# One transfer for each token tile of the first half, and tile 1's statistics ahead of tile 0's normalization

## The chip, the core and the metric

The kernel runs on one NeuronCore of one Trainium2 chip. The core has a matrix engine (TensorE, PE in the profile; its weight loads are the row PEld), a vector engine (VectorE, DVE), an activation engine (ScalarE, ACT), a general engine (GpSimd, POOL) and a queue engine that only issues transfers (SyncE, SP). ACT and POOL can issue transfers too. All transfers run on 16 shared DMA engines between HBM and SBUF, the on-chip memory of 128 partitions. PSUM holds matmul results. Every engine works through its own list in order; between engines there are semaphores. The metric is device time of one execution in microseconds (us), the median of the runs.

## What is computed

The input `x` has 2048 tokens of 576 values. Each token is normalized, and the result goes through two branches that are added to `x`: a long convolution whose kernel comes from a state-space model, and a feed-forward block with 4608 hidden units.

```python
x = A_u                                   # (1, 2048, 576)
xn = _layernorm(x, axis=-1)               # (x - mean) / sqrt(var + 1e-5), no weights
return x + _A_ref(xn, A_re, A_im, B_re, B_im, C_re, C_im, log_dt, Dskip) + _B_ref(xn, w1, w2)

def _B_ref(x, w1, w2):
    h = jnp.einsum("bsd,df->bsf", x, w1)  # 576 -> 4608
    h = _silu(h)
    return jnp.einsum("bsf,fd->bsd", h, w2)

# _A_ref: K[d, l] = Re sum_n C * exp(dt * A * l) * dt * B, for l = 0..2047;
#         y = causal convolution of xn with K along the tokens (by FFT), plus xn * Dskip
```

All of it is fp32. The kernel splits each operand of a matmul into a high and a low part (`h` and `l` in the names) and takes three products.

## The kernel before

**Tokens.** The tokens stand in 16 tiles of 128, tile j being `x` at 16 values of the rest. On the way in, tile j puts token 64n + 32·q2 + 16·q1 + j on partition 32·(2·q1 + q2) + n. The views `xv` and `ov` have that layout in four quarters of 32 partitions, so a load (`load_x`) or a store (`store`) of a tile, or of a pair of tiles, is four transfers of 32 partitions. The convolution's first stage needs just this order of the partitions: it reads the normalized tokens back from the DRAM buffer `dxn` (`xr<-dxn` in `spread`, line 146), and `dxn` is filled from the `xn` tiles by GpSimd (line 240). The feed-forward branch treats each token alone and needs no order.

**Stages.** `ffn` is the main stream. For half 0 (tiles 0 to 7) and half 1 (tiles 8 to 15) it runs over 9 chunks of four 128-wide pieces of the hidden units: `up` (lines 311 to 313, `ph`) makes 512 tokens by 128 hidden units, ScalarE applies silu (`gf`, line 319) and casts the high part (`gh`, line 320), VectorE makes the low part (`gl`, line 321), and `down` (line 341, `po`) multiplies by w2; VectorE adds the result into `acc` (line 346). `acc` of a tile is the loaded tile itself, so the residual is in it. Most of half 1 runs in a form with fewer products (line 468). `side` is woven between: it normalizes the tiles, prepares the state-space tables (`natural`, `kgen`; inputs `are`, `aim`, `cr` and so on), spreads the tokens (`spread`), multiplies in the transformed domain (`spectral`) and ends the convolution.

**The first 50 us.** Tile 0 and tile 1 are loaded by eight transfers, from SP and ACT in turn. `norm` takes statistics on VectorE (`st`, line 188; `mv`, line 189), adds 1e-5 to the variance (`sd`, line 192), GpSimd raises that to the power -1/2 (line 193), and VectorE or, for odd tiles from 5 on, ScalarE (line 202) writes `xn`. `turned` transposes `xn` on TensorE (`pt`, lines 122 and 127), and ScalarE and VectorE split the transposed tile into `xh`/`xl` (lines 123 and 125) and the small `x` piece (lines 128 and 129). Tiles 0 to 3 are block 0, tiles 4 to 7 block 1. An `up` product of a block reads all of that block's columns, except that the first one is cut into two halves of 256 columns, tiles 0 and 1 first. The tiles `xn` live in a pool `pa`, which is closed after tile 7: whatever is allocated there next, above all the state-space inputs `dt`, `are`, ... (loaded by SP from line 684 on), waits until the transfers out of `xn` have landed and TensorE has read the last tile.

**What sets the order.** Each engine's order is made when the program is built: a scheduler places the instructions by a simulated timeline, in the order of the code as `weave` mixes it and with `tc.high_priority()` ahead. `behind(ins)` places an instruction on its engine after another one. The first transfers of SP and ACT share eight completion semaphores; a ninth such transfer is issued only when the first has landed, and so on round. GpSimd's transfers have eight of their own.

```python
for i in range(n):
    for h in range(2):
      with behind(pins["xn"] if js[0] == 1 else None):
        nc.vector.bn_stats(out=st[:, i, h, :], in_=xs[i][:, h * HD:(h + 1) * HD])
```

So tile 1's statistics stand behind `pins["xn"]`, the instruction that writes tile 0's `xn`.

## Time and profile before

| | |
|---|---|
| median of 3 runs | 1107.37 us (1106.05 to 1108.47) |
| profiled execution | 1108.0 us, its span 1106.1 us (the rest lies around the span) |
| TensorE busy | 1089.5 us, 98% |
| TensorE weight loads | 986.5 us, 89% |
| VectorE busy | 950.6 us, 86% |
| ScalarE busy | 722.6 us, 65% |
| GpSimd busy | 141.5 us, 13% |
| HBM read / written | 109.64 MB / 62.60 MB |
| granted TensorE clock | 0.999 |

The span runs from the first instruction to the last. A row of the timeline has the start in us, the length in us, the engine (SPq and ACTq are the queues that issue transfers), the line, the operation, output<-input, and in brackets how long the engine had been idle and what ended that. In a table of stretches, each engine's busy time is followed by its number of instructions; then come the clock, the DMA engines' busy share and GB/s. A row of waits says who waited for whom: us in total, times, and the longest.

### The profile page before, as it was taken

Reading aid. Unit: us, or ns where it says so; the run is one execution under the profiler, and the core shown is the slowest. Engines: PE = TensorE matmul, PEld = TensorE weight load, DVE = VectorE, ACT = ScalarE, POOL = GpSimd, SP = SyncE. Lnnn points to the kernel's source line nnn. Section 1 sums busy time; section 2 is a strip of 40 time slices with the busy share of each in tenths; the row PEclk is TensorE's granted clock in tenths of the full one; section 3 lists DMA queues with packets and bytes.
Section 4 is the critical chain, followed back from the end, with each engine's and each line's share of the span. In section 5 each row is a group of like instructions: output and inputs, shape, how many; then the busy total and the mean of one; then the engine's idle time right before and its main releaser. Section 6 shows DMA issues by size and latency. Waiting matters only on the chain.

```text
span 1106.1 us, 23074 instructions
## 1 busy us (share of the span) xinstructions
PE 1089.5 (98%) x9101; PEld 986.5 (89%) x9101; DVE 950.6 (86%) x1615; ACT 722.6 (65%) x1283; POOL 141.5 (13%) x246
## 2 busy tenths in 40 slices
PE   6999999999999999999999999999999999999998
PEld 5989999898998888898999899999999998999787
DVE  6699989999999999999999997988888888886323
ACT  4475457677777676767667656877778777785320
POOL 1112100000000000000330001111111111111220
PEclk9999999999999999999999999999999999999999
DMA  8536552355263535457974246456545655554984
GB/s 261 157 123 205 168 165 94 118 149 153 84 176 108 138 125 132 154 120 254 240 196 89 84 92 193 146 167 179 158 152 176 182 173 150 177 161 109 248 216 111
DMA packets 163100, 173.67 MB, mean 157 GB/s; under 512 B 88608, under 2 KB 128816, under 8 KB 162352
## 3 DMA queue, kind: packets, MB, share of 16 engines
q1 hardware_dynamic: 137360, 105.02, 34.6%
q0 software_dynamic: 24272, 65.38, 19.4%
q10 hardware_dynamic: 1360, 1.80, 0.7%
q8 instruction: 72, 1.18, 0.5%
q14 instruction: 36, 0.29, 0.1%
HBM read 109.64 MB, written 62.60 MB: 156 GB/s over the span
## 4 chain that ended last, share of the span: by engine, by line
PE 78%; DVE 12%; ACT 3%; DMA 3%; issue 2%; SPq 0%; POOL 0%; ACTq 0%; DVEq 0%
PE po L341 34%; PE ph L311 16%; PE pb L468 6%; PE pc L468 3%; PE kp L888 2%; PE pk L1022 2%; PE pb L1022 2%; PE pu L1022 2%; PE pa L468 2%; PE ph L313 1%; PE ph L312 1%; PE z L903 1%; DMA kl<-d1k 1%; DVE acc L346 1%; DVE th L829 1%
## 5 line engine op out<-in xcount | busy, mean ns | idle before, releaser
L341 PE MATMUL po<-w,gh 128*128 128x288 f32 x2304 | 474.3, 296 | 0.7 <-DVE acc L346 0.7
L341 PEld LDWEIGHTS po<-w,gh 128*128 128x128 f32 x2304 | 375.1, 188 | 16.6 <-issue 3.3
L341 PE MATMUL po<-w,gl 128*128 128x288 f32 x1152 | 333.5, 295 | 0.0
L341 PEld LDWEIGHTS po<-w,gl 128*128 128x128 f32 x1152 | 214.9, 188 | 1.7
L346 DVE TENSOR_TENSOR acc<-po,acc 128x288 f32<-128x288 f32 x296 | 129.8, 451 | 54.5 <-PE po L341 53.2
L311 PE MATMUL ph<-xh,w1h 128*128 128x512 f32 (+1 forms) x368 | 99.7, 388 | 1.4 <-ACT gf L319 1.0
L311 PE MATMUL ph<-xl,w1h 128*128 128x512 f32 (+1 forms) x368 | 98.2, 384 | 0.0
L311 PE MATMUL ph<-xh,w1l 128*128 128x512 f32 (+1 forms) x368 | 98.0, 383 | 0.0
L319 ACT ACTIVATE gf<-ph 128x512 f32<-128x512 f32 (+1 forms) x92 | 53.0, 579 | 51.3 <-PE ph L313 31.5
L311 PEld LDWEIGHTS ph<-xl,w1h 128*128 128x128 f32 x368 | 68.0, 191 | 13.4
L311 PEld LDWEIGHTS ph<-xh,w1l 128*128 128x128 f32 x368 | 66.6, 189 | 12.0
L311 PEld LDWEIGHTS ph<-xh,w1h 128*128 128x128 f32 x368 | 65.0, 191 | 11.7 <-ACT gf L319 1.6
L845 ACT ACTIVATE c<-th,magic 128x1040 f32<-128x1040 f32 x36 | 42.0, 1168 | 40.6 <-DVE C L866 26.5
L159 POOL DMA_DIRECT2D d1u<-u x32 | 17.6, 550 | 393.9 <-ACT u L158 392.5
L847 ACT ACTIVATE c<-th 128x1040 f32<-128x1040 f32 x36 | 38.7, 1074 | 40.7 <-DVE th L846 40.6
L321 DVE TENSOR_TENSOR gl<-gf,gh 128x512 fp32r<-128x512 f32 (+1 forms) x92 | 60.3, 658 | 3.8 <-ACT gh L320 3.6
L927 POOL DMA_DIRECT2D m<-in_cm_dram x64 | 34.0, 533 | 216.0 <-PE pu L1022 135.8
L320 ACT CAST gh<-gf 128x512 fp32r<-128x512 f32 (+1 forms) x92 | 55.1, 602 | 8.7 <-PE po L341 7.7
L485 DVE TENSOR_TENSOR gl<-gf,gh 128x512 fp32r<-128x512 f32 x56 | 37.8, 688 | 23.4 <-ACT gh L484 23.0
L865 DVE TENSOR_TENSOR S<-th,C 128x1024 f32<-128x1024 f32 x36 | 43.8, 1218 | 7.4 <-ACT th L848 7.3
L846 DVE SCALAR_TENSOR_TENSOR th<-c,th 128x1040 f32<-128x1040 f32 x36 | 44.3, 1232 | 0.3 <-ACT c L845 0.3
L829 DVE TENSOR_TENSOR th<-vt,fT 128x1040 f32<-128x1040 f32 x36 | 44.3, 1233 | 0.2
(269 smaller groups left out, 2371.0 us busy)
## 6 DMA issues: line engine op xcount, KB each, us to landing
w1r<-in_B_w_dram SPq DMA_DIRECT2D x35, 512.0 KB, 3.9
dw<-w SPq DMA_DIRECT2D x28, 576.0 KB, 4.8
w<-dw POOLq DMA_DIRECT2D x28, 576.0 KB, 5.9
w2r<-in_B_w_dram SPq DMA_DIRECT2D x44, 288.0 KB, 4.8
d1u<-u POOLq DMA_DIRECT2D x32, 288.0 KB, 2.9
d1k<-stage SPq DMA_DIRECT2D x18, 512.0 KB, 6.5
ul<-d1u SPq DMA_DIRECT2D x32, 288.0 KB, 3.0
kl<-d1k SPq DMA_DIRECT2D x32, 288.0 KB, 3.6
```

Source lines behind the costliest of these rows:

```text
L311: nc.tensor.matmul(ph, w[:, kt, :], v[:, kt, a:e], start=n + kt == 0, stop=False)
L319: nc.scalar.activation(gf, ph, AF.Silu)
L320: pins["gh"] = nc.scalar.copy(gh, gf).ins
L321: pins["gl"] = nc.vector.tensor_sub(gl, gf, gh).ins
L341: pins["pe"] = nc.tensor.matmul(po[:, :HD], gs[g][:, js], ws[:, w, hs], start=n == 0 and j not in begun, stop=n == 3 * len(terms) - 1, ski ...
L346: nc.vector.tensor_add(acc[j][:, hs], po[:, :HD], acc[j][:, hs])
L468: pins["pe"] = nc.tensor.matmul(dst, a[:, kt], v[:, kt], start=start and n == 0, stop=stop and n == 5, skip_group_check=True).ins
L829: nc.vector.tensor_mul(split(th), row(vt[:, 0:65], 65), col(fT, i, 65))
L845: nc.scalar.activation(c65, th, AF.Identity, bias=magic)
L846: nc.vector.scalar_tensor_tensor(th, c65, MAGIC, th, op0=ALU.subtract, op1=ALU.subtract)
L865: nc.vector.tensor_mul(ov3, t[:, :, 0:64].rearrange("n d (x y) -> n d x y", y=32), mv3)
L1022: nc.tensor.matmul(dst, st, mv[:, hs], start=n == 0, stop=n == 3 * len(terms) - 1)
```

## The change

- Tiles 0 to 7 get another layout, `xw` and `ow`: partition p of tile j holds token 16p + j. A load of tile 0 or 1, and of each pair (2, 3), (4, 5), (6, 7), is then one transfer of 128 partitions, and so is each store of those pairs at the end of half 0. Tile 0 comes by SP, tile 1 by ACT. Tiles 8 to 15 keep the quarters.
- Since `dxn` keeps its order of partitions, the copy of `xn` of these tiles into `dxn` becomes four transfers of 32 partitions, each from every fourth partition of `xn`.
- Tile 1's statistics stand behind `pins["var"]`, the instruction that adds 1e-5 to tile 0's variance.

```diff
+    xw = x.rearrange("b (p j) d -> p (b j) d", j=NJ)
+    ow = out.rearrange("b (p j) d -> p (b j) d", j=NJ)
...
         t = pool.tile([P, 2, D], F32, tag=tag, name=f"{tag}{j}")
-        for i in range(j, j + 2, 1 if j == 0 else 2):
+        if j == 0:
+            for i, eng in enumerate(engines):
+                eng.dma_start(t[:, i], xw[:, i])
+        elif j < 8:
+            nc.sync.dma_start(t, xw[:, j:j + 2])
+        else:
             for ps, v, eng in quarters(xv, engines):
-                if j == 0:
-                    eng.dma_start(t[ps, i], v[:, i])
-                else:
-                    eng.dma_start(t[ps], v[:, j:j + 2])
+                eng.dma_start(t[ps], v[:, j:j + 2])
...
-              with behind(pins["xn"] if js[0] == 1 else None):
-                nc.vector.bn_stats(out=st[:, i, h, :], in_=xs[i][:, h * HD:(h + 1) * HD])
+                with behind(pins["var"] if js[0] == 1 else None):
+                    nc.vector.bn_stats(out=st[:, i, h, :], in_=xs[i][:, h * HD:(h + 1) * HD])
...
-        nc.vector.tensor_scalar(sd[:, :n], mv[:, :n, 1], 1e-5, None, op0=ALU.add)
+        pins["var"] = nc.vector.tensor_scalar(sd[:, :n], mv[:, :n, 1], 1e-5, None, op0=ALU.add).ins
...
-        held.append((dxn[:, js[0]:js[0] + len(js)], xn[:, :len(js)]))
+        ds = dxn[:, js[0]:js[0] + len(js)]
+        if js[0] < 8:
+            held.extend((ds[32 * q:32 * q + 32], xn[2 * (q % 2) + q // 2::4, :len(js)]) for q in range(4))
+        else:
+            held.append((ds, xn[:, :len(js)]))
...
-                    store(pairs[j - 1], j - 1, (nc.gpsimd,))
+                    nc.gpsimd.dma_start(ow[:, j - 1:j + 1], pairs[j - 1])
```

The order of the instructions moves with it on every engine, since the scheduler places them anew. Line numbers of the changed kernel are up to 9 higher than those before. Three places follow.

On VectorE, at the very start, the rows of tile 0 and tile 1 before (`st`, `mv`, `sd`, `xn` as above; `acc_104` is the pair of tiles 0 and 1):

```order
L188 BN_STATS st<-acc_104 128x6 x2
L189 BN_AGGR mv<-st 128x2
L192 TENSOR_SCALAR sd<-mv 128x1
L197 TENSOR_SCALAR xn<-acc_104,mv,sd 128x576
L188 BN_STATS st<-acc_104 128x6 x2
L189 BN_AGGR mv<-st 128x2
```

and with the change:

```order
L193 BN_STATS st<-acc_104 128x6 x2
L194 BN_AGGR mv<-st 128x2
L197 TENSOR_SCALAR sd<-mv 128x1
L193 BN_STATS st<-acc_104 128x6 x2
L202 TENSOR_SCALAR xn<-acc_104,mv,sd 128x576
L194 BN_AGGR mv<-st 128x2
```

The two statistics of tile 1 have moved ahead of tile 0's `xn`; the rest stands as it was.

On TensorE, at the end of block 0's first `down` products, where tile 7 is transposed (`pt`; the row of 64x128 is its last piece) and block 1's first `up` product (`ph<-xh`) follows, before:

```order
L122 MATMUL pt<-ident,xn 128x128 x4
L341 MATMUL po<-w_240,gh 128x288 x2
L341 MATMUL po<-w_240,gl 128x288
L341 MATMUL po<-w_243,gh 128x288 x2
L127 MATMUL pt_338<-ident,xn 64x128
L341 MATMUL po<-w_243,gl 128x288
L341 MATMUL po<-w_246,gh 128x288 x2
L341 MATMUL po<-w_246,gl 128x288
L341 MATMUL po<-w_249,gh 128x288 x2
L341 MATMUL po<-w_249,gl 128x288
L311 MATMUL ph<-xh_273,w1h 128x512 x8
```

and with the change:

```order
L350 MATMUL po<-w_246,gh 128x288 x2
L350 MATMUL po<-w_246,gl 128x288
L350 MATMUL po<-w_249,gh 128x288 x2
L350 MATMUL po<-w_249,gl 128x288
L125 MATMUL pt<-ident,xn 128x128 x4
L130 MATMUL pt_335<-ident,xn 64x128
L320 MATMUL ph<-xh_270,w1h 128x512 x8
```

Before, twelve products stood between the four large transposes of tile 7 and block 1's first `up`; now only the small transpose does.

On GpSimd, the transfers out of `xn` between the powers (`sd`) of the pairs, before:

```order
L193 TENSOR_TENSOR sd<-sd,mhalf 128x2
L240 DMA dxn<-xn 128x576 x2
L240 DMA dxn<-xn 128x1152
L193 TENSOR_TENSOR sd<-sd,mhalf 128x2 x2
L240 DMA dxn<-xn 128x1152 x2
```

and with the change:

```order
L198 TENSOR_TENSOR sd<-sd,mhalf 128x2
L249 DMA dxn<-xn 32x576 x8
L249 DMA dxn<-xn 32x1152 x4
L198 TENSOR_TENSOR sd<-sd,mhalf 128x2 x2
L249 DMA dxn<-xn 32x1152 x8
```

Five transfers have become twenty, twelve of them ahead of the powers of tiles 4 to 7.

## The prediction

> **What bounds the kernel now.** I read the page's busy times first, then a table of stretches to find where TensorE is not busy, then the timeline and the waits at those places.

> ```profile
> PE 1089.5 (98%) x9101; PEld 986.5 (89%) x9101; DVE 950.6 (86%) x1615; ACT 722.6 (65%) x1283; POOL 141.5 (13%) x246
> ...
> 0.00:12.00 12.00, 3.58 (x14) 2.67 (x15) 5.34 (x17) 4.50 (x9) 2.05 (x7) 1.00 0.72 204
> 12.00:30.00 18.00, 16.90 (x125) 16.22 (x125) 16.15 (x42) 9.51 (x24) 2.62 (x4) 1.00 1.01 294
> 62.00:80.00 18.00, 17.45 (x104) 15.57 (x103) 17.41 (x30) 13.66 (x16) 4.17 (x5) 1.00 0.42 140
> 300.00:400.00 100.00, 99.14 (x1076) 88.93 (x1075) 97.76 (x143) 70.84 (x105) 3.79 (x7) 1.00 0.52 148
> ```

> TensorE is the bound. It idles 16.6 us of 1106.1 (span less 1089.5): 8.4 in the first 12, 1.1 from 12 to 30, 0.55 from 62 to 80, 0.86 from 300 to 400. So the change can gain at most a part of the first 8.4, and what it delays counts only where TensorE then stands. From 300 to 400 VectorE has 2.2 us of air in 100: a wait there would reach TensorE soon.

> **The start, part by part.** This is the chain up to the first `up` product.

> ```profile
> 0.75 1.79 SPq L169 DMA_DIRECT2D acc<-in_A_u_dram  x4
> 3.37 0.40 SPq L257 DMA_DIRECT2D w1r<-in_B_w_dram  x1
> ...
> 4.29 0.82 DVE L188 BATCH_NORM_STATS2 st<-acc 128x6 f32<-128x288 f32 x2 [3.36 <-DMA acc<-in_A_u_dram]
> 5.39 0.15 DVE L192 TENSOR_SCALAR sd<-mv 128x1 f32<-128x1 f32 x1
> 6.24 0.58 DVE L197 TENSOR_SCALAR xn<-acc,mv,sd 128x576 f32<-128x576 f32 x1 [0.69 <-POOL sd L193]
> 6.73 0.81 DVE L188 BATCH_NORM_STATS2 st<-acc 128x6 f32<-128x288 f32 x2
> 7.58 0.21 DVE L189 BATCH_NORM_AGGREGATE mv<-st 128x2 f32<-128x12 f32 x1
> 8.66 0.58 DVE L197 TENSOR_SCALAR xn<-acc,mv,sd 128x576 f32<-128x576 f32 x1 [0.68 <-POOL sd L193]
> 9.59 0.72 ACT L279 CAST w1h<-w1r 128x640 fp32r<-128x640 f32 x1 [0.82 <-DMA w1r<-in_B_w_dram]
> 10.45 0.59 ACT L123 CAST xh<-pt 128x512 fp32r<-128x512 f32 x1
> 11.08 0.58 PE L311 MATMUL ph<-xh,w1h 128*128 128x256 f32 x1 [0.46 <-ACT xh L123]
> ```

> *Load.* Tile 0 is there just before 4.29. One transfer of 288 KB does not stand in this trace at this place; the nearest row is `xr<-dxn`, which also reads 128 rows of 2304 bytes with the same step of 36,864 bytes. The rows below it are DMA rates: the quarters of tiles 0 and 1, the quarters of tiles 2 and 3 (10.5 to 12.5 us), and whole 128-partition loads of w2 (13.5 to 15.5).

> ```profile
> DMA to landing us min/median/max: 2.7/3.7/10.8
> ...
> 1.50:4.50 3.00, 0.00 (x0) 0.00 (x0) 0.21 (x1) 1.19 (x2) 0.50 (x1) 1.00 0.78 221
> 10.50:12.50 2.00, 1.54 (x7) 1.42 (x7) 1.37 (x3) 2.00 (x5) 0.00 (x0) 1.00 0.95 249
> 13.50:15.50 2.00, 2.00 (x13) 2.00 (x13) 2.00 (x5) 0.00 (x0) 0.00 (x0) 1.00 1.03 338
> ```

> Early end: the 2.7 us, so tile 0 lands at 0.75 + 2.7 = 3.45. Late end: tile 1's 295 KB goes through at the same time from the other queue; at 221 GB/s that adds 1.33 us, so 4.78. If the median 3.7 holds instead of 2.7, it is 5.78. Against a landing of about 4.15 now, that is 0.7 earlier, 0.6 later, or 1.6 later. I take the middle of the first two, 4.1: the whole loads of w2 move faster (338) than quarters (249), which speaks for the early half, and the sharing for the late one. So the load as such gives 0.07.

> [...]

> *Statistics.* With 0.07 off, tile 0's variance is done at 5.47 (5.39 + 0.15 - 0.07). Tile 1's statistics, 0.81, run from 5.49 to 6.30 while GpSimd takes the power; it is done for VectorE at 6.17. Tile 0's `xn` so starts at 6.34 instead of 6.24, a loss of 0.1 that nothing waits for, since tile 1 is the later one. After it, at 6.95, tile 1's aggregation starts, 0.63 before its 7.58, and all behind it moves by 0.63: `xn` to 8.03, `xh` to 9.82, the first `up` to 10.45.

> *Weights.* ScalarE casts `w1h` between the two `xh`, and that cast waited for w1 until 9.59. It must start by 9.1. Its load stood behind the landing of a quarter (issued at 3.37, when a semaphore of the eight came free); with two transfers ahead instead of eight it needs no free semaphore and is issued some 2 us earlier on SP. I count that as enough; if w1 came no earlier, the gain would be 0.1.

> The start: -0.6 us, between -1.3 (early end) and +1.0 (5.78, less the 0.63).

> **Tile 7's transposes and the release of the pool.**

> ```profile
> 42.12 0.60 PE L122 MATMUL pt<-ident,xn 128*128 128x128 f32 x4
> 42.76 0.59 ACT L123 CAST xh<-pt 128x512 fp32r<-128x512 f32 x1 [2.59 <-PE pt L122]
> 43.53 0.26 ACT L128 CAST x<-pt 64x128 fp32r<-64x128 f32 x1 [0.18 <-PE pt L127]
> 43.57 0.31 SPq L684 DMA_DIRECT2D dt<-in_A_log_dt_dram  x1
> 44.26 2.00 PE L311 MATMUL ph<-xh,w1h 128*128 128x512 f32 x8
> 49.35 0.95 DVE L702 TENSOR_TENSOR aim<-aim,dt 96x768 f32<-96x768 f32 x1 [1.18 <-ACT aim L701]
> 51.13 0.41 PE L680 MATMUL ptk<-ident,aim 96*128 96x96 f32 x3
> ...
> SPq L684 <- DMA dxn<-xn: 8.0, 2, 6.6
> SPq L684 <- PE pt L127: 5.8, 1, 5.8
> ```

> Now twelve products run while ScalarE casts tile 7's `xh` (42.76 to 43.35). With the new order only the small transpose does, so `ph<-xh` stands still from about 42.75 to 43.39 of this clock: +0.6 us (0.5 to 0.7). Start and this cancel: TensorE begins block 1 at 44.26 as before.

> The release moves more. SP's `dt` load waits for two things, last of all for the read of tile 7: by the two rows the last `dxn` had landed 5.8 us before the transpose was done, at about 37.6. The cast of the small piece (43.53) then comes right behind `xh`, which ends 0.04 before 44.26, so `dt` goes out at about 44.2, 0.65 later. `aim` is ready for TensorE at 50.95 instead of 50.30, and wanted at 51.13: covered, with 0.18 left.

> ```profile
> 62.70 0.68 DVE L321 TENSOR_TENSOR gl<-gf,gh 128x512 fp32r<-128x512 f32 x1
> 63.31 0.95 DVE L730 TENSOR_TENSOR pi<-pi,t 96x768 f32<-96x768 f32 x1
> 64.29 0.85 ACT L733 ACTIVATE ci<-pi 96x768 f32<-96x768 f32 x1 [1.86 <-DVE pi L730]
> ...
> 77.63 1.20 PE L311 MATMUL ph<-xh,w1h 128*128 128x512 f32 x4 [0.56 <-ACT gf L319]
> ```

> From `ci` ScalarE works without a gap until the `gf` for which TensorE waits 0.56 at 77.63, so this chain carries the delay. But the new order has `pi` ahead of that `gl`: +0.65 - 0.61 = 0.04. So 77.63 stays where it is.

> **Transfers on GpSimd.** Fifteen more issues; the nearest price is that of 32-partition loads on the same queue.

> ```profile
> 17.87 1.99 POOL L240 DMA_DIRECT2D dxn<-xn  x3
> 17.95 1.07 DVE L197 TENSOR_SCALAR xn<-acc,mv,sd 128x576 f32<-128x576 f32 x2 [0.21 <-POOL sd L193]
> 30.07 1.62 POOL L193 TENSOR_TENSOR sd<-sd,mhalf 128x2 f32<-128x2 f32 x2 [10.21 <-DVE sd L192]
> 33.84 0.54 POOL L240 DMA_DIRECT2D dxn<-xn  x1 [0.32 <-ACT xn L202]
> ...
> L178 POOL DMA_DIRECT2D out_dram<-yt x16 | 12.6, 1208 | 33.8 <-ACT yt L991 33.8
> L171 POOL DMA_DIRECT2D acc<-in_A_u_dram x16 | 7.8, 495 | 15.1 <-DMA out_dram<-acc 15.1
> ...
> dxn<-xn POOLq DMA_DIRECT2D x2, 288.0 KB, 5.2
> ```

> Twelve from 17.87 at 0.5 end at 23.9; the next power is wanted at 30.07: hidden by 6 us. Eight from 33 end at 37, and with 5.2 to land at 42.2, before the release at 44.2. The cost is nothing while that cover of 2 us holds; the dearer price, 1.2 us of `yt`, is a rival below. At the end of half 0, twelve store issues fewer and whole loads elsewhere free queues that TensorE doesn't wait for: nothing.

> **Sum.** -0.6 + 0.6 + 0.04, and nothing for the new order behind 80 us, where the ends are -0.86 (the one idle there goes) and the +3.4 of the second rival: 0.0. The profiled execution took 1108.0, 1.9 more than its span and 0.6 more than the median; I forecast 1107.4 against the median 1107.37. A measurement of this kernel tells about 0.2%, 2.2 us, from no change. With the start's ends, this case reaches from 1105.8 (early end, and the idle of 300 to 400 gone) to 1109.0 (the latest landing).

> **Rivals.**
> 1. *The copies hold the release* (slower). If a 32-partition copy out of `xn` cost GpSimd the 1.2 us of `yt` (the same bytes and partitions), twelve would end at 32.4, 2.3 after the power at 30.07; eight more from 35.2 end at 44.9 and land at 50.1, 5.9 after 44.2. SP, VectorE and ScalarE would carry that to 77.63: 1113.3. It decides from a price of 0.75 us on (33 + 8 x 0.75 + 5.2 = 44.2). For it: `yt`'s price. Against: 0.495 for plain loads, 0.54 at 33.84, and `yt` accumulates. [...]
> 2. *The new order starves VectorE in the middle* (slower). Every engine's order after 80 us is new. If the 500 us from 140 to 640, where the tables keep VectorE full, each lost 0.86 per 100 as 300 to 400 does, that would be 4.3 instead of 0.86: +3.4, 1110.8. For it: 97.76 of 100. Against: the same work by the same scheduler. It decides from 2.2 lost.
> 3. *The start keeps its gain* (faster). Early end, -1.3; loads that move at 338 instead of 249 also take the 1.1 of 12 to 30 and the 0.55 of 62 to 80 with them; tile 7 still costs 0.6: -2.35, 1105.0. For it: DMA share 1.01 from 12 to 30. Against: TensorE's waits there are for VectorE and ScalarE, and 62 to 80 hangs on the release.

> **How the numbers follow.** No change that can be told: 0.62. Rival 1: 0.08, rival 2: 0.15, rival 3: 0.15. So faster 0.15, same 0.62, slower 0.23. The range 1105.0 to 1110.8 runs to rivals 3 and 2; rival 1 and the tails beyond the two, about 0.2, stay out.

> **What would show it.** Right: the first `up` at about 10.4, tile 1's statistics at 5.5 inside GpSimd's power, a TensorE idle of 0.6 ahead of block 1's `ph` caused by ScalarE's `xh`, `dt` at 44.2, and again about 0.5 idle at 77.6. Wrong: statistics of tile 0 later than 4.9 or earlier than 3.6; `dt` waiting last for `dxn`; copies above 0.75 us; more than 2 us of TensorE idle between 80 and 1000.

## The result, and the profile after

| | median us | lowest to highest | ratio to before |
|---|---|---|---|
| before, beside it | 1107.74 | 1106.05 to 1108.47 | |
| changed | 1115.51 | 1114.86 to 1116.43 | 1.0066 (1.0054 to 1.0079) |

The change makes the kernel 7.8 us slower. The forecast of 1107.4, with a range up to 1110.8, was wrong.

The profiled execution took 1115.5 us; its span is 1113.8, that is 7.7 more than before. First the busy times and the table of stretches of the changed kernel (busy time and number of instructions by engine, the granted clock of TensorE, the DMA engines' share, GB/s).

```profile
PE 1091.1 (98%) x9101; PEld 987.1 (89%) x9101; DVE 951.6 (85%) x1615; ACT 722.7 (65%) x1283; POOL 143.6 (13%) x249
...
0.00:12.00 12.00, 4.22 (x17) 3.24 (x18) 5.87 (x18) 5.00 (x10) 2.04 (x7) 1.00 0.88 263
12.00:30.00 18.00, 16.91 (x133) 16.22 (x133) 16.05 (x43) 9.78 (x25) 8.76 (x15) 1.00 0.87 269
30.00:80.00 50.00, 48.41 (x298) 43.57 (x297) 39.22 (x78) 32.15 (x46) 10.25 (x15) 1.00 0.40 128
80.00:140.00 60.00, 59.56 (x370) 53.76 (x369) 51.61 (x97) 29.19 (x50) 11.08 (x12) 1.00 0.56 183
140.00:240.00 100.00, 97.74 (x945) 87.54 (x944) 94.23 (x142) 64.73 (x94) 2.17 (x4) 0.98 0.43 127
300.00:400.00 100.00, 98.00 (x952) 87.72 (x951) 95.88 (x142) 68.37 (x103) 4.32 (x8) 1.00 0.50 147
400.00:680.00 280.00, 278.57 (x2905) 250.78 (x2904) 265.52 (x389) 185.31 (x278) 26.63 (x50) 1.00 0.51 142
680.00:1000.00 320.00, 318.95 (x2021) 296.02 (x2021) 277.89 (x535) 251.85 (x543) 58.63 (x110) 1.00 0.56 171
```

TensorE's idle time is 22.7 us (1113.8 less 1091.1), before it was 16.6: 6.1 of the 7.7. The other 1.6 is in its busy time, although it does the same work. By stretch: the first 12 us have 0.64 less idle, as forecast; up to 80 us the sum is 0.4 more (10.46 against 10.07); from 80 to 680 us it is 6.1 where before it was 0.9; behind that little changes (1.05 against 0.78 from 680 to 1000). The stretch from 80 to 680 us, before and then changed:

```profile
80.00:680.00 600.00, 599.14 (x5829) 540.53 (x5828) 572.30 (x868) 394.88 (x598) 52.18 (x90) 1.00 0.51 145
```

```profile
80.00:680.00 600.00, 593.86 (x5773) 533.98 (x5772) 564.79 (x852) 387.98 (x586) 46.37 (x78) 1.00 0.49 142
```

4.7 of the 6.1 lie ahead of 500 us. The change's own loads and copies are all issued by 37 us, and its mid stores (the stores of tiles 0 to 7 at the end of half 0) stand from 534 to 570 us. So most of the loss lies where the change itself does nothing. TensorE's longest waits in the changed kernel from 30 us on (who waited for whom: us, times, longest):

```profile
PE po L350 <- DVE acc L355: 4.7, 5, 1.8
PE ph L320 <- ACT gf L328: 1.0, 1, 1.0
PE po L350 <- DMA w<-dw: 0.8, 1, 0.8
PE ph L320 <- ACT xh L126: 0.6, 1, 0.6
```

and the same pair before:

```profile
PE po L341 <- DVE acc L346: 0.7, 1, 0.7
```

`po` products wait until VectorE has added an earlier `po` into `acc`, since that frees its buffer in PSUM (`po` has three). The longest of these waits, VectorE's rows and then TensorE's, in the changed kernel:

```profile
158.60 0.68 DVE L859 TENSOR_TENSOR C<-pw,al 128x512 f32<-128x512 f32 x1
159.20 0.68 DVE L875 SCALAR_TENSOR_TENSOR S<-th,C 128x512 f32<-128x512 f32 x1
159.80 1.22 DVE L874 TENSOR_TENSOR S<-th,C 128x1024 f32<-128x1024 f32 x1
160.94 1.18 DVE L355 TENSOR_TENSOR acc<-po,acc 128x288 f32<-128x288 f32 x3
...
161.44 0.54 PE L350 MATMUL po<-w,gh 128*128 128x288 f32 x2 [1.78 <-DVE acc L355]
```

and VectorE's rows before, at the same step of the tables (`C` and `S` are tables of the convolution's kernel):

```profile
159.52 0.68 DVE L850 TENSOR_TENSOR C<-pw,al 128x512 f32<-128x512 f32 x1
160.12 0.45 DVE L346 TENSOR_TENSOR acc<-po,acc 128x288 f32<-128x288 f32 x1
160.49 0.68 DVE L866 SCALAR_TENSOR_TENSOR S<-th,C 128x512 f32<-128x512 f32 x1
161.09 1.22 DVE L865 TENSOR_TENSOR S<-th,C 128x1024 f32<-128x1024 f32 x1
162.22 0.45 DVE L346 TENSOR_TENSOR acc<-po,acc 128x288 f32<-128x288 f32 x1
```

Before, one `acc` stood between `C` and the two `S` and the others behind them; now all three stand behind, and TensorE, which has nothing else next in its row, waits 1.78 us for the two `S`. VectorE has no less air than before. Its rows stand in another order. And the wait costs twice, as the clock shows (the column behind the busy times):

```profile
161.00:162.00 1.00, 0.56 (x4) 0.57 (x5) 1.00 (x4) 0.00 (x0) 0.00 (x0) 1.00 0.29 66
162.00:163.00 1.00, 1.00 (x8) 1.00 (x8) 1.00 (x4) 0.00 (x0) 0.00 (x0) 0.84 0.00 0
163.00:164.00 1.00, 1.00 (x6) 1.00 (x6) 1.00 (x2) 0.00 (x0) 0.00 (x0) 0.50 0.00 0
...
165.00:166.00 1.00, 1.00 (x6) 1.00 (x6) 1.00 (x3) 0.44 (x1) 0.00 (x0) 0.50 0.00 0
166.00:167.00 1.00, 1.00 (x9) 1.00 (x9) 0.70 (x3) 0.00 (x0) 0.00 (x0) 0.96 0.00 0
```

For 3.4 us behind the idle TensorE runs at half its clock: 0.16 + 3 x 0.50 + 0.04 = 1.7 us lost while busy, which agrees with the 1.6 more of busy time. This one wait costs 3.5 us.

The start of the changed kernel, for the steps of the prediction, and then the place of tile 7 and the `ph` of 77 us:

```profile
4.55 0.82 DVE L193 BATCH_NORM_STATS2 st<-acc 128x6 f32<-128x288 f32 x2 [3.62 <-DMA acc<-in_A_u_dram]
5.72 0.81 DVE L193 BATCH_NORM_STATS2 st<-acc 128x6 f32<-128x288 f32 x2
8.06 0.58 DVE L202 TENSOR_SCALAR xn<-acc,mv,sd 128x576 f32<-128x576 f32 x1 [0.68 <-POOL sd L198]
8.92 0.73 ACT L288 CAST w1h<-w1r 128x640 fp32r<-128x640 f32 x1
9.85 0.58 ACT L126 CAST xh<-pt 128x512 fp32r<-128x512 f32 x1 [0.20 <-PE pt L125]
10.49 1.22 PE L320 MATMUL ph<-xh,w1h 128*128 128x256 f32 x4 [0.42 <-ACT xh L126]
...
42.71 0.27 PE L130 MATMUL pt<-ident,xn 128*64 128x128 f32 x1
42.91 0.59 ACT L126 CAST xh<-pt 128x512 fp32r<-128x512 f32 x1 [2.44 <-PE pt L125]
43.06 0.31 SPq L693 DMA_DIRECT2D dt<-in_A_log_dt_dram  x1
43.39 0.26 ACT L131 CAST x<-pt 64x128 fp32r<-64x128 f32 x1
...
43.55 2.11 PE L320 MATMUL ph<-xh,w1h 128*128 128x512 f32 x8 [0.57 <-ACT xh L126]
77.47 0.95 PE L320 MATMUL ph<-xh,w1h 128*128 128x512 f32 x3 [1.02 <-ACT gf L328]
```

The first `up` comes at 10.49 (forecast 10.45), tile 7 costs 0.57 (forecast 0.6), `dt` is issued at 43.06 (forecast 44.2), and the `ph` at 77.47 waits 1.02 (forecast about 0.5).

### The profile page after: what moved, and what is told of

Read it like the earlier page. It is cut to its first block, busy times and chain, and to the rows that moved or that the text cites. A ratio compares the mean times of both kernels' runs of the same rounds, so it can differ in the third digit from the quotient of the medians.

```text
span 1113.8 us, 23075 instructions
## 1 busy us (share of the span) xinstructions
PE 1091.1 (98%) x9101; PEld 987.1 (89%) x9101; DVE 951.6 (85%) x1615; ACT 722.7 (65%) x1283; POOL 143.6 (13%) x249
## 3 DMA queue, kind: packets, MB, share of 16 engines
q8 instruction: 72, 1.18, 0.4%
## 5 line engine op out<-in xcount | busy, mean ns | idle before, releaser
L874 DVE TENSOR_TENSOR S<-th,C 128x1024 f32<-128x1024 f32 x36 | 43.9, 1220 | 10.2 <-ACT th L857 10.1
## 6 DMA issues: line engine op xcount, KB each, us to landing
w2r<-in_B_w_dram SPq DMA_DIRECT2D x44, 288.0 KB, 4.6
d1u<-u POOLq DMA_DIRECT2D x32, 288.0 KB, 3.0
ul<-d1u SPq DMA_DIRECT2D x32, 288.0 KB, 2.8
kl<-d1k SPq DMA_DIRECT2D x32, 288.0 KB, 3.3
```

The source lines that it names most:

```text
L874: nc.vector.tensor_mul(ov3, t[:, :, 0:64].rearrange("n d (x y) -> n d x y", y=32), mv3)
```

## The experiments

Theory O says that the re-placed order of the instructions costs the time: nothing that the change does on the chip is dear, but the scheduler puts the rows of the next 600 us elsewhere. Theory W says that the work costs it: the copies on GpSimd, the whole loads, the whole mid stores, and buffers that come free at other times. Theory S says that the early statistics upset the start. The split between them needs kernels in which the order and the work part company. That can be arranged, since each engine's order is fixed when the program is built and can be compared row by row. Some ways of writing the same change leave TensorE's 5195 rows exactly as before, and some edits that have nothing to do with the change move them.

| | part of the change | TensorE's order | median us (before beside it) | ratio, 95% | idle 80 to 680 us | lost at half clock |
|---|---|---|---|---|---|---|
| before | none | its own | | | 0.9 | 0 |
| changed | all | another from row 75 on | 1115.51 (1107.74) | 1.0066 (1.0054 to 1.0079) | 6.1 | 1.7 |
| e1 | statistics | as before | 1107.63 (1108.31) | 0.9993 (0.9985 to 1.0002) | 1.0 | 0 |
| e2 | layout, mid stores in four pieces | as before | 1108.27 (1108.31) | 1.0002 (0.9993 to 1.0011) | 3.1 | 0 |
| e3 | all, copies and mid stores in other pieces | as before | 1108.00 (1108.31) | 0.9999 (0.9990 to 1.0008) | 1.0 | 0 |
| e4 | all, copies in other pieces | as before to row 2600 | 1107.79 (1108.31) | 0.9993 (0.9984 to 1.0002) | 1.2 | 0 |
| e5 | all, mid stores in four pieces | as changed to row 2600, as before from 3400 | 1114.42 (1107.86) | 1.0052 (1.0040 to 1.0065) | 5.0 | 1.7 |
| e6 | none | as e5 from row 500 | 1113.92 (1107.86) | 1.0050 (1.0038 to 1.0063) | 5.9 | 0 |
| e7 | none | a third from 524 to 3400 | 1111.09 (1107.86) | 1.0023 (1.0013 to 1.0032) | 4.1 | 0 |
| e8 | all | as changed to row 1000, a fourth to 3400 | 1117.59 (1107.86) | 1.0083 (1.0069 to 1.0096) | 6.6 | 1.7 |
| e9 | as e3 | as before from row 280 | 1108.98 (1109.12) | 1.0003 (0.9994 to 1.0012) | 2.7 | 0 |

The last two columns, TensorE's idle time and its loss behind an idle that halved the clock, are in us, from one profiled execution of each. The ratio and its interval are those on record; the ratio differs a little from the quotient of the medians, and the losses below go by the ratio.

### e1: the statistics alone

```diff
-              with behind(pins["xn"] if js[0] == 1 else None):
+              with behind(pins["var"] if js[0] == 1 else None):
```

> The kernel before with the one line on tile 1's statistics (they stand behind tile 0's variance); loads, copies and stores as before. PE's and ScalarE's order is that of before in every row, VectorE's differs in the place of one `xn`. Theory O (the loss of 7.8 us is the re-placed order behind 80 us, above all `po` products that wait for VectorE's `acc`, not any work of the change): the first `up` moves by 0.1 us only, since `w1h` still waits for w1 until 9.59; total 1107.2, between 1106.2 and 1108.2. Theory W (the work of the change, its transfers, costs the time): nothing here of it, 1107.2 as well. Theory S (the early statistics themselves upset the start): 1110 or more.

Measured: no change. The first `up` comes at 10.67, 0.41 earlier than before instead of 0.1: w1 was there a little sooner (its cast at 9.41 instead of 9.59), and the second `xh` followed it at 10.04. At 78.07 TensorE waits 0.84 for `gf` (before 0.56 at 77.63), so that the start's gain is gone by there. Theory S falls.

### e2: the layout alone

All of the layout, with `pins["xn"]` kept, and the mid stores in four pieces:

```diff
-                    nc.gpsimd.dma_start(ow[:, j - 1:j + 1], pairs[j - 1])
+                    for q in range(4):
+                        ps = slice(32 * q, 32 * q + 32)
+                        nc.gpsimd.dma_start(ow[ps, j - 1:j + 1], pairs[j - 1][ps])
```

> The layout with all its transfers (whole loads of tiles 0 to 7, the sixteen 32-partition copies on GpSimd), tile 1's statistics where they were before, and the mid stores in the new layout but as four transfers of 32 partitions, as many as before. PE's order is that of before in every row. Theory O: no `po` waits over 0.7 us from 80 to 680, total 1107 give or take 1.5 (the start gives 0 to 0.6, nothing is lost behind). Theory W: the copies and whole loads cost here what they cost in the changed kernel, 1111 to 1116. Theory S: 1107, as theory O.

Measured: no change, with the same twenty copies and whole loads as in the changed kernel. Theory W falls for these. One expectation was missed: the profiled execution has a wait of 0.81 for `acc` at 353.65 (before 0.67 there) and one of 1.41 for `w1h` at 128.28, whose piece of w1 could be cast 6.5 us after the issue of its load (127.50 against 121.05), before 4.3. That execution took 1110.87, the longest of eleven; its 3.1 us of idle are not the kernel's usual ones. By itself the layout makes the start slower: tile 0 is there at 4.74 instead of 4.29, and the first `up` comes at 11.53, 0.45 later.

### e3: both parts, in the old order

The mid stores as in e2, and the copies in another cut:

```diff
-            held.extend((ds[32 * q:32 * q + 32], xn[2 * (q % 2) + q // 2::4, :len(js)]) for q in range(4))
+            dv = dxn.rearrange("(b a r) n d -> b r a n d", b=2, a=2)
+            held.extend((dv[b, :, :, j], xn[b::2, i]) for i, j in enumerate(js) for b in range(2))
```

> Both parts of the change at once, but written so that PE's order is that of before in every row: the copies of tiles 0 to 7 are sixteen of 64 partitions and one tile each instead of sixteen of 32 partitions (four of them with one tile's 2304 bytes a row doubled), the mid stores four transfers of 32 partitions. Theory O: the first `up` at 10.5 us, no idle ahead of block 1's `ph` since tile 7's transposes stand where they stood, so the 0.6 us of the start is kept up to there; total 1106.8, between 1105.5 and 1108.0. Theory W: 1111 to 1116. Theory S: 1110 or more.

Measured: 0.9999 of before. This is the change without its loss. The stretch from 80 to 680 us:

```profile
80.00:680.00 600.00, 598.97 (x5832) 540.75 (x5831) 571.99 (x868) 394.91 (x599) 52.00 (x90) 1.00 0.50 145
```

Two things differ from the changed kernel beside the order, the pieces of the copies and of the mid stores; e2 has the copies of 32 partitions without a loss, e4 the whole mid stores. The start of e3 is the best of all (first `up` at 10.43, 0.65 earlier than before), and no idle stands ahead of block 1's `ph`. Even so nothing is won. VectorE's first product of `cr` and `br`, and the `ph` of 77 us, in e3:

```profile
51.87 0.96 DVE L737 TENSOR_TENSOR pr<-cr,br 96x768 f32<-96x768 f32 x1 [2.16 <-DMA cr<-in_A_C_re_dram]
...
77.67 1.20 PE L321 MATMUL ph<-xh,w1h 128*128 128x512 f32 x4 [0.93 <-ACT gf L329]
```

Before, `pr` stood at 51.84. The 0.34 us by which `dt` was issued earlier end in the wait for `cr`; from there to 63.3 VectorE has no gap, ScalarE carries it on, and the `ph` comes at 77.67 as before at 77.63, with the gain turned into idle (0.93 against 0.56).

### e4: the mid stores as in the change

The copies as in e3, the mid stores one transfer per pair.

> As the run before it, but the mid stores are one transfer per pair as in the changed kernel. PE's order is that of before up to its row 2600 (some 500 us) and re-placed behind it. Theory O: idle of PE from 80 to 500 us as before (under 1.5 us; the changed kernel has 4.7); what the re-placed order from 500 on costs is open by the theory, between -1 and +4 us (the changed kernel has 3.4 us of idle between 500 and 1090, before 0.8): 1106 to 1111. Theory W with the mid stores as the cause: 1111 to 1116 with waits from 640 us on.

Measured: 0.9993, 1.2 us of idle from 80 to 680. The order behind row 2600 is another than that of before and costs nothing. So a re-placed order need not be dear, and the whole mid stores are not the cause.

### e5: the changed kernel, mid stores in four pieces

After e1 to e4 one rival was left, theory C: the full change as written acts on the chip through its transfers and buffers, and the order as such is worth little.

The diff of e2 on the changed kernel.

> The changed kernel with one thing put back: the mid stores of tiles 0 to 7 as four transfers of 32 partitions each. PE's order is that of the changed kernel up to its row 2600 (some 500 us) and, from row 3400 on, that of before. Theory O (the re-placed order costs the time, wherever it stands): the stretch from 80 to 500 us keeps its 4.7 us of idle and the half clock near 163 us; what the changed kernel lost behind 500 us beyond the kernel before (3.4 us of idle against 0.8) goes: total 1112 to 1114. Theory C (early transfers and buffers on the chip cost it, the order is worth under 1 us): 1114 to 1116, as the changed kernel. If the mid stores were the cause: 1107 to 1109.

Measured: 1114.42, 0.4 above the range of theory O; the places agree. TensorE waits 1.76 at 161.74 with the half clock behind it, and 1.69 at 358.60, as in the changed kernel; from 400 to 680 us it isn't idle at all.

```profile
161.74 0.53 PE L350 MATMUL po<-w,gh 128*128 128x288 f32 x2 [1.76 <-DVE acc L355]
...
358.60 0.53 PE L350 MATMUL po<-w,gh 128*128 128x288 f32 x2 [1.69 <-DVE acc L355]
```

The remaining loss, 5.8 us (1.0052), stands with the order from row 75 to 3400.

### e6: the kernel before, two loads exchanged

```diff
-        br, bi = load(b_re, "br"), load(b_im, "bi")
-        cr, ci = load(c_re, "cr"), load(c_im, "ci")
+        br, cr = load(b_re, "br"), load(c_re, "cr")
+        bi, ci = load(b_im, "bi"), load(c_im, "ci")
```

> The kernel before with none of the change; the table loads of c_re and b_im change places (dt, are, aim, br, cr, bi, ci instead of br, bi, cr, ci). PE's order from its row 500 (some 110 us) to the end is then, row by row, that of the run before this one. Theory O: the same `po` waits for `acc` as there, 1.8 near 160 us with the half clock behind it and 1.7 near 358, in a kernel that has no part of the change: 1111 to 1114. Theory C: 1106.5 to 1109.

Measured: 1113.92. A kernel with nothing of the change loses 5.5 us (1.0050), as e5 does, once it has e5's order:

```profile
110.72 0.53 PE L341 MATMUL po<-w,gh 128*128 128x288 f32 x2 [1.13 <-DVE acc L346]
...
162.58 0.54 PE L341 MATMUL po<-w,gh 128*128 128x288 f32 x2 [1.09 <-DVE acc L346]
...
358.11 0.53 PE L341 MATMUL po<-w,gh 128*128 128x288 f32 x2 [1.70 <-DVE acc L346]
```

The wait at 358 is that of e5 to 0.01 us. The one near 162 is shorter (1.09 instead of 1.76, with waits of 0.41 and 0.40 ahead of it at 147.27 and 155.47) and has no half clock behind it, which I had expected; a wait of 1.13 at 110.72 makes up for part. The exchange of the loads costs nothing by itself at its own place: up to 80 us TensorE idles 9.4 us, before 10.1. Theory C, by which the order is worth under 1 us, falls. Together with e3, which has the change and no loss in the old order, this shows the order as the cause.

### e7: the kernel before, another mark

```diff
-        marks = (0.1357, 0.613, 0.855)
+        marks = (0.1340, 0.613, 0.855)
```

> The kernel before with none of the change; the first mark, the share of the products at which the tables of the convolution begin, is 0.1340 instead of 0.1357. PE's order is that of before up to row 524 and from row 3400 on, and another one between, neither that of before nor that of the changed kernel. Theory O: the time leaves before by more than 0.2%, likely upward, by waits of `po` for `acc` in 140 to 640 us: 1110 to 1116. Theory C: 1106.5 to 1109.

Measured: 1111.09, 2.5 us (1.0023). The size agrees with theory O, the waits do not: for `acc` only 0.3, and that outside 80 to 680 us, but 2.1 for ScalarE's cast of w2, 1.0 for its cast of w1, 0.7 for `sp`. So it is not always `acc`; an order has its own waits. The 1.0 (at 127.45) may be none of the order's: e2 and e9 wait there too (1.41 and 1.01), for a late landing of w1, and have the old order at that place.

### e8: the changed kernel, another mark

`marks` begins with 0.1375, the change is complete.

> The changed kernel, all parts of the change as they are, with the first mark at 0.1375. PE's order up to about row 500 is that of the changed kernel, another one between, and from row 3400 that of before. Theory O: the time differs from the changed kernel by the waits that this order has, and lies anywhere between 1106 and 1114, with the sum of `po` waits for `acc` from 80 to 680 us saying where. Theory C: 1114 to 1117, as the changed kernel.

Measured: 1117.59, which is outside what theory O gave and near what theory C gave. Taken alone it would speak for C, which e6 rules out. The places speak for O: up to row 1000 (the text above says 500) the order is that of the changed kernel, and up to 224 us the waits for `acc` are too (1.77 at 162.12, with the half clock); behind it there are others (for ScalarE's `gh` 1.12 at 420.53 and 1.53 at 546.56 instead of 1.70 for `acc` near 358). The upper end I gave had no rows behind it and was too low.

### e9: `cr` from another queue

e3, with the load of `cr` issued by GpSimd, to see whether the start's gain can be kept past 51.87.

```diff
-        cr, ci = load(c_re, "cr"), load(c_im, "ci")
+        cr, ci = load(c_re, "cr", nc.gpsimd), load(c_im, "ci")
```

> Both parts of the change in the old order (third run), and the load of c_re issued on GpSimd's queue instead of as the sixth on SP's; PE's order differs from before in 26 of 5195 rows, all ahead of row 280 (about 80 us). Theory K (the 0.6 us that the start gains ends where VectorE waits 2.2 us for the load of cr at 51.9, a wait that the start doesn't move, and shows as idle of 0.93 at 77.67): `pr` starts up to 1 us earlier, the idle near 77.7 falls below 0.5, and the total is 0.4 to 0.9 below the third run, a ratio to before of 0.999 to 0.9995. Rival B (the seven loads are limited by what the queues move, so that another of them comes later by as much): the idle near 77.7 stays at 0.8 to 1.0, ratio 1.000.

Measured: 1.0003. The rival's numbers hold:

```profile
50.20 0.95 DVE L737 TENSOR_TENSOR pr<-cr,br 96x768 f32<-96x768 f32 x1 [2.38 <-DMA br<-in_A_B_re_dram]
...
77.48 1.19 PE L321 MATMUL ph<-xh,w1h 128*128 128x512 f32 x4 [0.87 <-ACT gf L329]
```

`pr` comes 1.67 earlier but now waits for `br`, the product of `aim` has moved from ahead of it to behind it on VectorE (0.87), and VectorE then stands 0.37 for ScalarE's `gh`. At 77.48 only 0.19 of it is left. So the stretch from 44 to 77 us is held by several things at once, and no version here beats the kernel before.

### e10 and e11: idle time and clock

Bursts of equal products, and between them idle times that one VectorE operation of a chosen length sets (in e11, 288 columns, a new weight load for each):

```python
for m in range(100 + (7 * n) % 23):
    nc.tensor.matmul(po[:, :288], w[:, m % 6], y[:, :288], start=True, stop=True)
nc.vector.tensor_copy(few, po[:, 0:1])
nc.vector.tensor_scalar(y[:, :size], xs[:, :size], few, None, op0=ALU.mult)
```

> Not the computation at all, a measurement of the granted clock: bursts of 58 to 70 equal products (13 to 16 us), and between them idle times of PE that one VectorE operation sets, of twelve lengths from about 0.9 to 3.6 us, each five times; the output holds a piece of the input. Theory L (the length alone decides, between 1.70 and 1.76 us as in the runs so far): no idle below 1.7 us is followed by half the clock, every one above 1.76 is. Theory F (a window that runs on its own decides, so the place of the idle in it counts): among equal lengths between 1.7 and 3.4 us some are followed by half the clock and others not.

> Not the computation, a second measurement of the granted clock, with the form of products that stood around the idle in the changed kernel: 288 columns and a new weight load for each, in bursts of 100 to 122 (some 13 to 16 us), and between them idle times in twelve lengths from about 1.4 to 2.2 us, each five times; the output holds a piece of the input. In the run before, 1.90 us never halved the clock (5 of 5) and 2.27 always did (4 of 4), while in the changed kernel 1.76 to 1.78 us did at one place (3 of 3) and 1.69 to 1.70 did not at another (4 of 4). Theory M (how full the products keep TensorE around the idle counts, so that with 288 columns a shorter idle is enough): here idles from about 1.75 us on are followed by half the clock. Theory F (the place in a window that runs on its own): some of the idles of equal length are, others not, between 1.7 and 2.2 us. If neither: none below 2.0 us is, as in the run before.

(The second text counts 4 of 4 at 1.69 to 1.70; the runs had 3.) In e10 no idle up to 1.64 us and none of the five of 1.90 halved the clock, and all four of 2.27 that had a burst behind them did. By length alone that is neither theory's; the last section comes back to it. In e11 equal idles part. Two of 1.80 us, and the clock of the 4 us around what follows each:

```profile
246.24 1.59 PE L38 MATMUL po<-y,w 128*128 128x288 f32 x9 [1.80 <-DVE y L40]
...
691.90 0.90 PE L38 MATMUL po<-y,w 128*128 128x288 f32 x5 [1.80 <-DVE y L40]
...
246.00:250.00 4.00, 3.76 (x19) 3.79 (x20) 0.09 (x1) 0.00 (x0) 0.00 (x0) 0.67 0.00 0
...
691.50:695.50 4.00, 3.60 (x27) 3.63 (x28) 0.25 (x1) 0.00 (x0) 0.00 (x0) 1.00 0.00 0
```

Up to 1.75 us none of the idles halved the clock, at 2.19 all four did, and of the 25 from 1.79 to 2.10 twelve did: theory F. What tells these apart is shown in the last section.

## Why the prediction was wrong, step by step

- *TensorE is the bound, and only its idle counts.* Right, with one addition: 1.7 us went in slower busy time, which no term of the sum had.
- *The start, -0.6.* The sum came out (11.08 to 10.49), in part by luck. I took 4.1 for the landing of tile 0, the middle; its statistics started at 4.55, nearer the late end. (The middle of 0.7 earlier and 0.6 later is 0.04 earlier, not the 0.07 I went on with; nothing hangs on it.) The layout alone costs the start 0.45 (e2), the statistics alone bring 0.41 (e1), where I had 0.1 without an earlier w1. Both bring 0.59: in e1 tile 1's statistics wait for its quarters until 5.76, with the whole loads they stand at 5.72, so a tile 0 that lands 0.26 later costs nothing; and w1, issued at 1.20 instead of 3.37, no longer holds the cast (8.92, in e1 9.41). The term on the weights was right.
- *The load's two ends, 3.45 and 4.78.* The transfers of tiles 0 and 1, issued side by side, took 3.8 and 4.0 us to land, so nearly together, as the late end has it. Why they do isn't shown: the first pieces of w1, issued at 1.20 and 1.26 on the same two queues, were under way at the same time. The late end was wrong even so: 4.55 is short of 4.78, and as said above it cost nothing. The early end, 2.7 us to land, did not come either.
- *Tile 7's transposes, +0.6.* Right: 0.57, for ScalarE's `xh`, and none in e3, where they stand as before. Still block 1 did not begin at 44.26 but at 43.55, since TensorE was busy 0.63 us less for the same products up to there (34.11 against 34.74); no term had that.
- *The release at 44.2, `ph` at 77.63 unmoved.* The first half failed. I let `dt` wait for ScalarE's cast of the small piece (43.39 in the changed kernel); it waits for TensorE's read of `xn`, as the prediction's own row `SPq L684 <- PE pt L127` has it, and goes out at 43.06, right behind the transpose. The second half came out for another reason: 77.47. What arrives earlier at 44 us waits for the tables' loads (e3).
- *Fifteen more issues on GpSimd, nothing.* Right. The copies took 0.54 each at the median; none of what followed was late, and with all twenty e2 loses nothing.
- *Rival 1, copies that hold the release.* Not so: 0.54 is below the 0.75 from which it decides.
- *The new order behind 80 us, 0, between -0.86 and +3.4.* This step failed, and it is nearly the whole miss. Measured: idle from 80 to 680 up by 5.3 and 1.7 of half clock, 7.0 of the 7.7. It is also the sign of being wrong that the prediction named: 7.2 us of idle between 80 and 1000, where more than 2 was the mark. I priced another order by the idle of the old one. That old order is a good one among those tried: five orders gave +0, +2.5, +5.5, +5.8 and +9.2 us (e4, e7, e6, e5, e8), and none measurably less than before. A `po` that finds two table operations ahead of its `acc` waits up to 1.8 us, so one such place outweighs the whole change; the bound had to be taken from such rows (0.68 + 1.22 + 0.45) times the places, not from 0.86 per 100 us.
- *Rival 2, the new order starves VectorE.* The right rival, at a chance of 0.15 and with too low a price. Its mechanism needs correcting: VectorE is not fuller, its rows stand differently, and in e7 it is ScalarE's rows.
- *Rival 3, the start keeps its gain.* No, not even in the old order (e3).

What made the scheduler re-place everything from row 75 on is not settled. The statistics alone, the layout alone, and both with copies of 64 partitions leave the rows there as they were; both with copies of 32 partitions do not. The first rows that differ are the transposes of tile 4: 48 `po` products stand ahead of them instead of 36 (34.27 and 34.12 us), and those of tile 7 are a later place of the same shift. Why the scheduler's timeline moves them was not traced.

## What to carry to other kernels

Where a scheduler sets the order, an edit of the first microseconds is two changes, what it does and where everything behind it now stands; here the second cost 7.0 us and the first brought 0.6 at the start, and a change that is neutral in the old order (e3) lost 0.7% by it. Before believing or rejecting such an edit, write it in a second way that keeps the old order, and make the new order once without the edit: the pair (here e3 and e6) tells in two runs which of the two it was. When forecasting, give the order its own term, with ends from the longest operations that can come to stand ahead of a wait, not from the idle of the old order.

## What was not expected of the hardware

An idle time of TensorE much shorter than the stretch of half clock behind it halved the clock: 1.78 us of idle, then 3.4 us at 0.50 in the changed kernel. Its length does not decide alone. In e11, with equal products around it, none of 30 idles up to 1.75 us was followed by half the clock, 12 of 25 between 1.79 and 2.10 were, and 4 of 4 of 2.19.

In the changed kernel and e5, 1.76 to 1.78 us were enough, a little over half of the period. Near this length the same wait cost 1.8 us or 3.5 (1.8 and 1.7 of half clock), by where it fell, as the two idles of 1.80 in e11 have it.
